# One plan and one pool layout for three phases that had one each, on one core

## The chip, the cores and the metric

The kernel runs on one core of a Trainium2 chip. The metric is device microseconds of one execution, from launch to end. The kernel before took 1201.57 us (median of 3 runs, 1199.39 to 1202.25). The engines are called TensorE (PE in the profile), VectorE (DVE), ScalarE (ACT), GpSimd (POOL) and SyncE (SP, which issues nearly all DMAs). Each engine takes its instructions strictly in the order in which the program lists them.

## The reference, cut to what matters

Linear attention with random features feeds a gated feed-forward layer. All is float32.

```
q, k, v: (8 batches, 8 heads, 576, 64);  omega: (128, 64);  q is scaled by 3.371
phi(x) = exp(h - max(h)) / sqrt(128),  h = (x/64**.25) @ omega.T - |x/64**.25|**2 / 2
kv  = phi(k).T @ v;   z = sum over positions of phi(k)
att = (phi(q) @ kv) / (phi(q) @ z + 1e-6)
x   = att as 4608 tokens x 512                       # 8 heads x 64
xn  = x / sqrt(mean(x*x) + 1e-6) * rms_g
g   = xn @ w_gate (512 x 1536);  val = xn @ w_val (512 x 1536)
out = (g * sigmoid(g) * val) @ w_out (1536 x 512)
```

## The kernel before, in words

**Number format.** The large products are made in three passes: each operand is split into a high part (a cast on ScalarE) and a low part (the difference, on VectorE or GpSimd), and TensorE adds high by high, high by low and low by high (`three_pass`, lines 147 to 154; `split`, `halve`). The weights come as 64-bit floats and are first put together from their two words (`weights` in phase A: one ScalarE and four VectorE steps for each of 36 pieces).

**Tiling.** The 4608 tokens are 36 chunks (`c`) of 128 and 12 blocks (`blk`) of 384. The 1536 hidden columns are 12 tiles (`f`) of 128.

**Phase A** (`phase_a`, lines 183 to 738) does the attention, and the first six `f` of gate and value. For each chunk `features` makes phi(k) and phi(q): load `ink` or `inq`, square and sum, project (`pjk`, `pjq`), maximum, exponentials into `kp` or `qp`. `kv_mid` and `kv_half` sum `kv`; `attend` transposes `qp` (`qt`), multiplies by `kv` (`nu`), divides, normalises, transposes (`xt`), stores the chunk in DRAM (`xn_d`, shown as `xn_scratch`) and splits it into `xT`. `gated(blk, f)` makes two products `ff` of 12 matmuls with 384 columns, gate and value, and three silu steps: `t` (tanh, ScalarE), `u` and `h` (VectorE). `u` frees the gate's PSUM bank and `h` the value's; there are two banks, so the next `ff` waits for them. `h` is stored in DRAM (`h_d`, shown as `h_scratch`). The weights of the other six `f` are combined and stored in DRAM (`lw_d`), those of `w_out` too (`wo_d`).

**Phase B** (`phase_b`, lines 741 to 970) does gate and value for the other six `f`, by a scheme with seven products in place of eight for each 2 by 2 group of blocks. `weights(un)` loads and splits seven left operands for each of six units `un` (`wr`, then `lw_un`); `tokens(bp)` loads four pieces of `xn_d` for a pair of blocks (`Xb`), takes four differences (`Xt`) and splits seven right operands (`R`); `unit` has seven products `p` of six matmuls and combines them (`c`, `u`).

**Phase C** (`phase_c`, lines 973 to 1017) multiplies all of `h_d` by `w_out`: per block and `f` a tile `hC` is loaded and split (`hh`, `hl`), and nine matmuls of 512 columns add to three banks `po`. In the first block each `w_out` tile is loaded (`oraw`, 4 buffers) and split (`ohi`, `olo`). 8 buffers for `hC`, 4 pairs for its split.

**What sets the order.** Phases A and B have a `Plan` each (lines 65 to 144): entries with an engine, an estimated duration, what they come after, a key, and the buffers that they take and give back. `order()` walks through time; a free engine takes the ready entry with the lowest key. An entry is ready 0.12 us after the last one that it needs (a DMA 2.2 us later still). `KEYS` holds the keys of the first nine chunks and the first weights. The silu steps of `gated` have the key `-1000 + 1000 + 6*blk + f`, so 0 to 71; a chunk's other steps have about its number `c`. Until the plan begins the first `ff`, a free TensorE gets `spin` matmuls. Phase C has no plan; its loop's order stands.

Each phase opens its buffers in pools of its own and closes them at its end; the next phase's pools lie in the same memory from the same end. The three lists are given to the framework under `manual_schedule` one after another (C's without it), and the framework itself places instructions of a later phase between those of an earlier one where memory and data allow.

Of the kernel before, what the change touches and what calls it, by code (L numbers as in the profile page):

```python
# [64 lines left out]
class Plan:  # L65
# [15 lines left out]
    def order(self):  # L81
# [25 lines left out]
        while len(out) < n + extra:  # L107
# [50 lines left out]
def performer_glu_kernel(  # L158
# [16 lines left out]
    with ExitStack() as ph:  # L175
        phase_a(ph, tc, qx, kx, va, vmid, omT, rmsg, wgv, wout, xn_d, h_d, lw_d, wo_d)
    with ExitStack() as ph:
        phase_b(ph, tc, lw_d, xn_d, h_d)
    with ExitStack() as ph:
        phase_c(ph, tc, wo_d, h_d, out)  # L180


def phase_a(ctx, tc, qx, kx, va, vmid, omT, rmsg, wgv, wout, xn_d, h_d, lw_d, wo_d):
    nc = tc.nc
    cpool = ctx.enter_context(tc.tile_pool(name="const", bufs=1))
# [11 lines left out]
    ve = nc.vector  # L197
    pools = {}
    slots = {}

    def pool(name, bufs, space=None, per=1):
        kw = {"space": space} if space else {}
        pools[name] = ctx.enter_context(tc.tile_pool(name=name, bufs=bufs * per, **kw))
        slots[name] = bufs

    psum = bass.MemoryType.PSUM
    wpool = ctx.enter_context(tc.tile_pool(name="wA", bufs=1))
    pool("xT", 2, per=2)
    for name, bufs in (
        ("t", 2), ("u", 2), ("h", 4), ("xr", 2), ("xn", 1), ("x", 1), ("qpT", 1), ("qp", 2),  # L210
        ("kv", 4), ("inq", 2), ("mag", 2), ("w", 4), ("sr", 1), ("f64", 2), ("ink", 3), ("v", 6),
        ("vm", 1), ("kp", 6),
    ):
        pool(name, bufs)
    pool("small", 16)
    pool("psJ", 4, psum)
    pool("psM", 2, psum)
    pool("psF", 2, psum)
    plan = Plan(slots)
    add = plan.add  # L220
    st = {}
# [10 lines left out]
    def weights(n, key):  # L232
# [65 lines left out]
        if n >= 2 * FA:  # L298

            st["wt", n] = t  # L300
            if n >= 2 * NF:
# [4 lines left out]
                i = add("SP", 0.26 / RATE, store, [i], key, land=LAND)  # L306
# [23 lines left out]
    def sums(n, key):  # L330
# [36 lines left out]
        ends.append(add("SP", 0.52 / RATE, store(2), after, key, land=LAND))  # L367
        add("NONE", 0, lambda: None, ends, give=[("w", n - 2), ("w", n), ("sr", un)])
# [163 lines left out]
    def attend(c, key):  # L532
# [126 lines left out]
        s = add("SP", 0.26 / RATE, xstore, [i], key - 0.3, land=LAND)  # L659
# [4 lines left out]
    def gated(blk, f, key):  # L664
# [34 lines left out]
        top = -1000 + key  # L699
# [9 lines left out]
        add("SP", 0.2 / RATE, store, [i], top, give=[("h", at)], land=LAND)  # L709
# [26 lines left out]
    with tc.manual_schedule():  # L736
        for begin in plan.order():
            begin()


def phase_b(ctx, tc, lw_d, xn_d, h_d):

    nc = tc.nc
    ve = nc.vector
    pools = {}
    slots = {}

    def pool(name, bufs, space=None, per=1):  # L750
        kw = {"space": space} if space else {}
        pools[name] = ctx.enter_context(tc.tile_pool(name=name + "B", bufs=bufs * per, **kw))
        slots[name] = bufs

    psum = bass.MemoryType.PSUM
    for name, bufs in (("s0", 2), ("s4", 2), ("u2", 2), ("u4", 2), ("u3", 2), ("g", 8), ("h", 6)):
        pool(name, bufs)
    lpool = ctx.enter_context(tc.tile_pool(name="lB", bufs=1))
    lw = {}
    for un in reversed(range(NU)):  # L760
        for i in range(7):
            for part in "hl":
                lw[un, i, part] = lpool.tile([P, 2, P], F32R, name=f"lw{un}_{i}{part}")
    names = ("b11", "b21", "b22", "t1", "t2", "t3", "t4")
    for nm in names:
        pool("R" + nm, 1, per=2)
    for nm in ("b11", "b21", "b22", "b12", "t1", "t2", "t4"):
        pool("X" + nm, 1)
    pool("wr", 2)
    pool("ps", 8, psum)  # L770
    plan = Plan(slots)
    add = plan.add
    st = {}

    def tile_(pool, shape, name, dtype=F32):
        return pools[pool].tile(shape, dtype, tag=pool, name=name)
# [12 lines left out]
    def weights(un, key):  # L789

        t = {}

# [10 lines left out]
        ld = add("SP", 0.39 / RATE, load(0, 3), key=key, take=[("wr", un)], land=LAND)  # L803
        ld = [ld, add("SP", 0.52 / RATE, load(3, 7), [ld], key, land=LAND - LAT)]
        ends = []
        for i, _ in ORDER:
# [6 lines left out]
                [ld[i > 2]],  # L813
# [6 lines left out]
    def tokens(bp, key):  # L820
# [3 lines left out]
        for nm, half, blk in (("b11", 0, 0), ("b12", 0, 1), ("b22", 1, 1), ("b21", 1, 0)):  # L824
# [5 lines left out]
            ld[nm] = add("SP", 0.39 / RATE, load, key=key, take=[("X" + nm, bp)], land=LAND)  # L830
# [41 lines left out]
    def unit(bp, fp, j, key):  # L872
# [31 lines left out]
        def plus(name, pool, x, y, eng=ve):  # L904
# [3 lines left out]

            return go

        out = "h" if j else "g"
        top = -1000 + key
        p = {}
        last = []
# [46 lines left out]
    for un in range(NU):  # L961
        weights(un, un)
# [120 lines left out]
```

## Time and profile before

| | |
|---|---|
| median of 3 runs | 1201.57 us |
| profiled execution, its own time | 1199.83 us |
| its span, first to last instruction | 1198.0 us |
| mean granted TensorE clock | 0.989 of full |
| TensorE busy | 1169.3 us, 98%, 7471 matmuls |
| VectorE busy | 731.4 us, 61% |
| ScalarE busy | 561.4 us, 47% |
| GpSimd busy | 193.8 us, 16% |
| DMA | 171.17 MB, 143 GB/s on average |
| first `ff` / last `ff` of phase A | 88.1 / 620.8 us |
| first `p` / last `p` of phase B | 624.3 / 890.1 us |
| first `po` / last `po` of phase C | 897.5 / 1193.4 us |

The slices of the profile (40 of 30 us) show TensorE busy 9 tenths or more nearly everywhere. The slices in which its granted clock is not full are those at 390, 540, 600, 870, 900 and 1170 us (0.89, 0.89, 0.94, 0.92, 0.96, 0.93). In the lists of groups, a line shows source line, engine, operation, output and inputs, count, busy time and mean ns, then idle time of the engine just before and who ended it. A matmul's duration is longer than its step to the next one, as matmuls are pipelined. SP is shown by the issue of its DMAs (SPq).

### The profile page before, as it was taken

The page shows a single profiled execution, that of the slowest core. Times are in us where ns is not written, and L with a number is a line of the kernel's source. Part 1 is how long each engine was busy: PE and PEld are TensorE (multiplying, and loading weights), DVE is VectorE, ACT ScalarE, POOL GpSimd, SP SyncE. Part 2 cuts the span into 40 slices and gives each one's busy share as a digit, 9 for nine tenths or more (in the row PEclk, how much of TensorE's full clock was granted, in tenths as well). Part 3 has the DMA queues.
Part 4 walks back from the last instruction along what each step waited for, and adds up shares of the span by engine and source line. Part 5 has one row for each costly group of instructions (what it writes and reads, how often), then busy time and mean ns, then how long its engine had stood idle before and what let it go on. Part 6 is the DMA issues. An engine that isn't in the chain of part 4 may idle for free.

```text
span 1198.0 us, 20303 instructions
## 1 busy us (share of the span) xinstructions
PE 1169.3 (98%) x7471; PEld 1079.6 (90%) x7471; DVE 731.4 (61%) x1483; ACT 561.4 (47%) x1382; POOL 193.8 (16%) x221
## 2 busy tenths in 40 slices
PE   9999999999999899998989999999979999999998
PEld 6889999999999899998989999999978888888886
DVE  5877898898888355456325878877755333333332
ACT  5778677766766345454226442442424222222221
POOL 0232121120101012110119422331310000000000
PEclk9999999999999899998999999999999999999999
DMA  8755487586664423223214322322137444444441
GB/s 296 227 169 174 151 266 256 196 260 210 228 206 163 138 80 111 80 85 117 74 40 156 100 86 93 104 83 85 54 104 238 126 125 121 133 143 121 124 125 67
DMA packets 98035, 171.17 MB, mean 143 GB/s; under 512 B 9360, under 2 KB 65552, under 8 KB 97936
## 3 DMA queue, kind: packets, MB, share of 16 engines
q1 hardware_dynamic: 97712, 169.58, 43.9%
q8 instruction: 59, 0.97, 0.3%
q10 hardware_dynamic: 224, 0.30, 0.1%
q14 instruction: 40, 0.33, 0.1%
HBM read 114.00 MB, written 55.84 MB: 142 GB/s over the span
## 4 chain that ended last, share of the span: by engine, by line
PE 48%; issue 3%; POOL 1%; DMA 0%; DVE 0%; ACT 0%; POOLq 0%; SPq 0%; ACTq 0%; DVEq 0%
PE po L152 8%; PE po L153 8%; PE po L154 8%; PE p L154 6%; PE p L153 6%; PE p L152 6%; PE ff L152 2%; PE ff L154 2%; PE ff L153 2%; POOL c L907 0%; DMA oraw<-wo_scratch 0%; PE nu L558 0%; POOL Rt2l L785 0%; DMA h_scratch<-h 0%; POOL Rt4l L785 0%
## 5 line engine op out<-in xcount | busy, mean ns | idle before, releaser
L152 PE MATMUL ff<-xhi,whi 128*128 128x384 f32 x576 | 204.1, 354 | 9.4 <-DVE u L685 9.4
L154 PE MATMUL ff<-xhi,wlo 128*128 128x384 f32 x576 | 194.7, 338 | 0.0
L153 PE MATMUL ff<-xlo,whi 128*128 128x384 f32 x576 | 194.6, 338 | 0.0
L57 DVE TENSOR_TENSOR hl<-hC,hh 128x384 fp32r<-128x384 f32 x144 | 80.2, 557 | 184.4 <-ACT hh L54 183.9
L152 PE MATMUL po<-ohi,hh 128*128 128x512 f32 x432 | 168.2, 392 | 7.0 <-ACT ohi L54 7.0
L153 PE MATMUL po<-olo,hh 128*128 128x512 f32 x432 | 168.1, 391 | 0.0
L154 PE MATMUL po<-ohi,hl 128*128 128x512 f32 x432 | 168.1, 391 | 0.0
L54 ACT CAST hh<-hC 128x384 fp32r<-128x384 f32 x144 | 74.3, 516 | 195.8 <-PE po L153 179.4
L152 PEld LDWEIGHTS ff<-xhi,whi 128*128 128x128 f32 x576 | 109.8, 191 | 11.7 <-DVE u L685 10.2
L153 PEld LDWEIGHTS ff<-xlo,whi 128*128 128x128 f32 x576 | 110.1, 191 | 0.0
L154 PEld LDWEIGHTS ff<-xhi,wlo 128*128 128x128 f32 x576 | 109.6, 190 | 0.0
L152 PEld LDWEIGHTS po<-ohi,hh 128*128 128x128 f32 x432 | 81.8, 190 | 24.5 <-ACT ohi L54 7.3
L153 PEld LDWEIGHTS po<-olo,hh 128*128 128x128 f32 x432 | 81.5, 189 | 17.0
L154 PEld LDWEIGHTS po<-ohi,hl 128*128 128x128 f32 x432 | 81.5, 189 | 16.9
L428 ACT ACTIVATE qp<-pjq,biq 128x128 f32<-128x128 f32 x288 | 88.2, 377 | 17.7 <-DVE biq L419 15.1
L428 ACT ACTIVATE kp<-pjk,bik 128x128 f32<-128x128 f32 x288 | 89.1, 378 | 15.4 <-DVE bik L419 14.9
L938 ACT ACTIVATE c<-c 128x384 f32<-128x384 f32 x72 | 37.6, 526 | 112.9 <-DVE c L907 95.7
L691 DVE SCALAR_TENSOR_TENSOR h<-u,ff 128x384 f32<-128x384 f32 x72 | 39.8, 552 | 56.1 <-PE ff L154 55.0
L681 ACT ACTIVATE t<-ff 128x384 f32<-128x384 f32 x72 | 35.6, 495 | 79.9 <-PE ff L154 79.7
L558 PE MATMUL nu<-kv,qpT 128*128 128x65 f32 (+1 forms) x640 | 71.6, 264 | 0.0
L558 PEld LDWEIGHTS nu<-kv,qpT 128*128 128x128 f32 (+1 forms) x640 | 69.0, 182 | 2.9 <-issue 0.9
L907 DVE TENSOR_TENSOR c<-p,u 128x384 f32<-128x384 f32 x108 | 58.9, 551 | 19.5 <-PE p L154 19.4
(145 smaller groups left out, 2364.2 us busy)
## 6 DMA issues: line engine op xcount, KB each, us to landing
hC<-h_scratch SPq DMA_DIRECT2D x144, 192.0 KB, 2.4
ink<-in_kx_dram SPq DMA_DIRECT2D x36, 512.0 KB, 4.5
inq<-in_qx_dram SPq DMA_DIRECT2D x36, 512.0 KB, 4.1
h_scratch<-h SPq DMA_DIRECT2D x72, 192.0 KB, 1.9
h_scratch<-c SPq DMA_DIRECT2D x72, 192.0 KB, 1.8
f<-in_wgv_dram SPq DMA_DIRECT2D x24, 512.0 KB, 4.6
xn_scratch<-xr SPq DMA_DIRECT2D x36, 256.0 KB, 2.7
Xb<-xn_scratch SPq DMA_DIRECT2D x24, 384.0 KB, 3.2
```

The lines of the kernel that those rows point to most:

```text
L54: nc.scalar.copy(hi, raw)
L57: lo_eng.tensor_tensor(out=lo, in0=raw, in1=hi.bitcast(F32), op=ALU.subtract)
L152: nc.tensor.matmul(out, lhsT=ah, rhs=bh, start=first, stop=False)
L153: nc.tensor.matmul(out, lhsT=ah, rhs=bl, start=False, stop=False)
L154: nc.tensor.matmul(out, lhsT=al, rhs=bh, start=False, stop=last)
L428: nc.scalar.activation(st[tag + "p", c][:, h, :], t["pts"][h % 2][:, h // 2, :], AF.Exp, bias=t["bi"][:, h : h + 1], scale=SCALE,)
L558: nc.tensor.matmul(pt[lo:hi, i, :], lhsT=t["qpT"][:, h, lo:hi], rhs=st["kv", b][:, h, :], start=True, stop=True,)
L681: nc.scalar.activation(t["t"], t[0], AF.Tanh, scale=0.5)
L691: ve.scalar_tensor_tensor(out=t["h"], in0=t["u"], scalar=0.5, in1=t[1], op0=ALU.mult, op1=ALU.mult)
L907: eng.tensor_tensor(out=t[name], in0=t[x], in1=t[y], op=ALU.add)
L938: nc.scalar.activation(t[nm], t[nm], AF.Silu)
```

## The change

One function with one plan holds all three phases. The pools are in groups (`GROUPS`); a group opens and closes by an entry of the plan on an engine of its own, `POOLS`, that takes no time. Groups named in `RIGHT` lie at the other end of SBUF.

- At the start `late`, `psA` (PSUM) and, on the other side, `early` are open. `early` has what the attention and the weights need (`f64`, `w`, `ink`, `inq`, `kp`, `qp`, `v`, ...), `late` what the silu steps and `xT` need.
- `to_b`, after the last user of `early`: `early` closes; `operands` (the seven `R`, and the left operands of unit 0, `lw0`) and `sources` (`X`, `wr`) open on the same side. B's loads and the splits of `R` and of unit 0 come after `to_b`.
- `in_b`, after all entries of A: `psA` and `late` close; `products` and `psB` open. The left operands of units 1 to 5 lie there.
- `to_c`, after the last user of `sources`: `first` opens (6 `hC` buffers, 3 pairs for its split, 2 for raw `w_out`, the split tile of `f` = 0). C's loads and these splits come after `to_c`.
- `in_c`, after all entries of A and B: `products` and `psB` close; the other split `w_out` tiles, the output buffers and `psC` open.

In phase C `wst` has 2 buffers (4 before), `hin` 6 (8), the split pairs 3 (4). C is planned too; its keys are `12000 + 12*blk + f`. B's keys begin at 6000. The silu steps get keys near -2000, below all others. The plan makes an entry ready at once when all that it needs ran on its own engine (and for `POOLS`). `KEYS` are new. The arithmetic and the shapes of all instructions stay.

```diff
-    "k": [-24.0, -20.7, -17.6, -7.8, -8.5, -5.1, 2.5, -6.7, 2.6],
-    "q": [-11.3, -7.1, 2.6, 2.9, 3.8, 3.9, 4.1, 4.6, 6.3],
-    "w": [
-        -1.5, -1.6, -2.7, 3.0, 6.2, 6.0, 6.5, 5.7,
-        11.7, 11.0, 13.1, 11.0, 34.5, 20.9, 13.7, 38.5,
-    ],
-    "lead": 6.14,
-    "v": 1.16,
-    "kv": 0.77,
-    "attend": -8.69,
+    "k": [-23.5, -21.2, -13.7, -12.7, -11.4, -10.9, -7.9, -5.4, -2.9],
+    "q": [-19.0, -9.9, -1.7, -1.2, 1.9, 4.5, 4.6, 5.1, 5.8],
+    "w": [-6.9, 1.8, -0.5, 3.1, 4.2, 4.5, 4.5, 4.7, 5.0, 5.2, 6.1, 9.3, 10.1, 6.5, 19.1, 35.5],
+    "lead": 4.94,
+    "v": 2.67,
+    "kv": -9.77,
+    "attend": -12.63,
 }
+GROUPS = {
...
+    "first": {"hin": (6, 1), "hs": (3, 2), "wst": (2, 1), "wo0": (1, 1)},
...
+RIGHT = ("early", "operands", "sources", "first")
...
-                if done < 0:
-                    continue
-                given.update(self.items[i][6])
-                for u in users[i]:
+                if done >= 0:
+                    given.update(self.items[i][6])
+                for u in users[i] if i >= 0 else ():
+                    at_once = self.items[u][0] in ("POOLS", self.items[i][0])
+                    if (at_once and (not self.items[i][7] or self.items[u][0] == "POOLS")) != (done < 0):
+                        continue
...
+    def change(after, old, new, then=lambda: None):
+        def go():
+            for group in old:
+                leave(group)
+            for group in new:
+                enter(group)
+            then()
+        return add("POOLS", 0, go, after)
...
-        top = -1000 + key
+        top = -3000 + key
...
+    to_b = change(users("early"), ["early"], ["operands", "sources"], lambda: left_tiles(0))
+    in_b = change(
+        list(range(to_b)),
+        ["psA", "late"],
+        ["products", "psB"],
+        lambda: [left_tiles(n) for n in range(1, NU)],
+    )
...
+        ready = to_b if un == 0 else in_b
...
-                [ld[i > 2]],
+                [ld[i > 2], ready],
...
+            after = [st["xs", NC * (2 * bp + blk) + i] for i in range(NC)] + [to_b]
+            ld[nm] = add("SP", 0.39 / RATE, load, after, key, [("X" + nm, bp)], land=LAND)
...
+    to_c = change(users("sources"), ["sources"], ["first"])
+    in_c = change(list(range(to_c)), ["psB", "products"], ["last", "psC"])
+    def out_weights(f, key):
...
+        ready = [in_c if f else to_c]
+        i = add("SP", 0.26 / RATE, load, [st["wo", f], to_c], key, [("wst", f)], land=LAND)
+        raw = lambda: t["raw"]
+        st["o", f] = halve("DVE", hi, lambda: hi("l"), raw, key, [i] + ready, DM, give=[("wst", f)])
...
+        i = add("SP", 0.2 / RATE, load, [st["hs", at], to_c], key, [("hin", at)], land=LAND)
+        i = halve("DVE", hi, lambda: t["l"], lambda: t["raw"], key, [i], TB, [("hs", at)], [("hin", at)])
+        take = [("psO", blk, c) for c in range(NC)] if f == 0 else []
+        before = [st["made"]] if "made" in st else []
+        i = add("PE", 2.06, product, before + [i, st["o", f], in_c], key, take, [("hs", at)])
```

## Rows read from the trace of the kernel before

**Rows 1.** Waits of TensorE: total us, times, longest us.
```profile
PE ff L152 <- DVE u L685: 9.4, 2, 5.4
```
**Rows 2.** Windows: length, busy us of PE, PEld, DVE, ACT, POOL; PEclk, DMA, GB/s.
```profile
405.00:410.00 5.00, 4.87 (x15) 4.87 (x16) 1.10 (x3) 0.01 (x1) 0.00 (x0) 0.50 0.11 39
```
**Rows 3.** Timeline of TensorE at 400: start, us, instruction [idle before <-releaser].
```profile
400.86 0.34 PE L154 MATMUL ff<-xhi,wlo 128*128 128x384 f32 x1
405.13 0.69 PE L152 MATMUL ff<-xhi,whi 128*128 128x384 f32 x1 [3.94 <-DVE u L685]
...
410.74 0.34 PE L154 MATMUL ff<-xhi,wlo 128*128 128x384 f32 x1
```
**Rows 4.** Timeline of TensorE at 550.
```profile
548.42 1.00 PE L558 MATMUL nu<-kv,qpT 128*128 128x65 f32 x8
554.84 0.69 PE L152 MATMUL ff<-xhi,whi 128*128 128x384 f32 x1 [5.42 <-DVE u L685]
...
560.88 0.36 PE L153 MATMUL ff<-xlo,whi 128*128 128x384 f32 x1
```
**Rows 5.** Timeline of TensorE from A to B.
```profile
620.84 0.34 PE L154 MATMUL ff<-xhi,wlo 128*128 128x384 f32 x1
624.33 0.45 PE L152 MATMUL p<-Rb11h,lw_0h 128*128 128x384 f32 x1 [3.15 <-ACT lw_0h L780]
...
631.34 0.33 PE L152 MATMUL p<-Rt2h,lw_4h 128*128 128x384 f32 x1
```
**Rows 6.** Timeline of TensorE from B to C.
```profile
890.13 0.34 PE L154 MATMUL p<-Rt4h,lw_2l 128*128 128x384 f32 x1
897.48 1.65 PE L152 MATMUL po<-ohi,hh 128*128 128x512 f32 x3 [7.02 <-ACT ohi L54]
...
905.97 0.39 PE L152 MATMUL po<-ohi,hh 128*128 128x512 f32 x1
...
908.01 0.39 PE L152 MATMUL po<-ohi,hh 128*128 128x512 f32 x1
```
**Rows 7.** Timeline of SP (issues) and of ScalarE, 390 to 404.
```profile
391.15 1.74 SPq L828 DMA_DIRECT2D Xb<-xn_scratch  x4
...
394.85 0.34 SPq L378 DMA_DIRECT2D inq<-in_qx_dram  x1
...
402.97 0.63 ACT L382 ACTIVATE inq<-inq 128x512 f32<-128x512 f32 x1 [4.38 <-DMA inq<-in_qx_dram]
```
**Rows 8.** Timeline of ScalarE, 543 to 551.
```profile
543.83 0.82 ACT L780 CAST Rb11h<-Xb 128x768 fp32r<-128x768 f32 x1
...
550.39 0.49 ACT L681 ACTIVATE t<-ff 128x384 f32<-128x384 f32 x1
```
**Rows 9.** Timeline of TensorE at 88, and the group of `spin` in the list by line.
```profile
88.16 0.42 PE L152 MATMUL ff<-xhi,whi 128*128 128x384 f32 x1
...
L713 PE MATMUL spin<-ones 128*128 128x512 f32 x135 | 42.8, 456 | 1.5 <-POOL ones L193 1.5
```
**Rows 10.** Tiles `u`, `Xb`, `lw_0l`: ns min/median/max, first and last start.
```profile
L685 DVE SCALAR_TENSOR_TENSOR u<-t,ff x72: 541/553/556, 92.1 to 617.6; 128x384 f32<-128x384 f32 x72
...
L785 DVE TENSOR_TENSOR Rb22l<-Xb,Rb22h x6: 948/2326/2331, 553.4 to 851.1; 128x768 fp32r<-128x768 f32 x6
...
L785 POOL TENSOR_TENSOR lw_0l<-wr,lw_0h x6: 732/738/741, 624.4 to 654.6; 128x256 fp32r<-128x256 f32 x6
```
**Rows 11.** Windows: the tail of A.
```profile
570.00:600.00 30.00, 30.00 (x184) 29.76 (x183) 10.72 (x21) 8.29 (x17) 5.33 (x7) 1.00 0.21 67
```
**Rows 12.** Tile `oraw`: its splits, and the landing of its loads.
```profile
L54 ACT CAST ohi<-oraw x12: 613/620/623, 896.8 to 912.5; 128x512 fp32r<-128x512 f32 x12
L57 DVE TENSOR_TENSOR olo<-oraw,ohi x12: 684/692/695, 897.5 to 913.1; 128x512 fp32r<-128x512 f32 x12
...
DMA to landing us min/median/max: 2.8/4.5/5.1
```
**Rows 13.** A weight's longest step in the list by line.
```profile
L272 DVE SCALAR_TENSOR_TENSOR w<-f,mag 128x512 int32<-128x512 int32 x36 | 27.5, 767 | 0.1
```

More of the change, by code (lines that the diff above doesn't have):

```diff
@@ L174, in performer_glu_kernel, with enter, leave, users @@
 ):
[L175 to L183, printed above, removed]
-    nc = tc.nc
-    cpool = ctx.enter_context(tc.tile_pool(name="const", bufs=1))
+    nc = tc.nc
+    ve = nc.vector
+    pools = {}
+    stacks = {}
+    plan = Plan({name: bufs for group in GROUPS.values() for name, (bufs, _) in group.items()})
+    add = plan.add
+    st = {}
+    def enter(group):
+        stack = stacks[group] = ExitStack()
+        side = "right" if group in RIGHT else "left"
+        space = {"space": bass.MemoryType.PSUM} if group.startswith("ps") else {}
+        for name, (bufs, per) in GROUPS[group].items():
+            pools[name] = stack.enter_context(
+                tc.tile_pool(name=name, bufs=bufs * per, side=side, **space)
+            )
+    def leave(group):
+        stacks.pop(group).close()
+    def change(after, old, new, then=lambda: None):
[6 more added lines that the diff above has]
+        return add("POOLS", 0, go, after)
+    def users(*groups):
+        names = {name for group in groups for name in GROUPS[group]}
+        return [
+            n for n, it in enumerate(plan.items) if any(t[0] in names for t in it[5] + it[6])
+        ]
+    for group in ("late", "early", "psA"):
+        enter(group)
+    cpool = wpool = pools["keep"]
     ident = cpool.tile([P, P], F32, name="ident")
@@ L196, in phase_a @@
     nc.scalar.dma_start(om[D:P, :], omT)
[L197 to L221, printed above, removed]
     def tile_(pool, shape, name, dtype=F32, tag=None):
@@ L735, in phase_a, with left_tiles @@
             gated(blk, f, 1000 + blk * FA + f)
[L736 to L758, printed above, removed]
     lw = {}
-    for un in reversed(range(NU)):
+    def left_tiles(un):
+        pool = pools["lw0" if un == 0 else "lw"]
         for i in range(7):
             for part in "hl":
[L763 to L776, printed above, removed]
+                lw[un, i, part] = pool.tile([P, 2, P], F32R, name=f"lw{un}_{i}{part}")
+    to_b = change(users("early"), ["early"], ["operands", "sources"], lambda: left_tiles(0))
[4 more added lines that the diff above has]
+        lambda: [left_tiles(n) for n in range(1, NU)],
+    )
     def halve(eng, hi, lo, raw, key, after, size, take=(), give=(), name=None):
@@ L787, in halve, with left @@
         return add(eng, dur, low, [h], key, give=give)
-    def weights(un, key):
+    def left(un, key):
         t = {}
+        ready = to_b if un == 0 else in_b
         def load(a, b):
@@ L869, in tokens @@
             st["R", bp, nm] = e
-            add("NONE", 0, lambda: None, [e] + [d[x] for x in users.get(nm, [])], give=[("X" + src, bp)])
+            add("NONE", 0, lambda: None, [e] + [d[x] for x in readers.get(nm, [])], give=[("X" + src, bp)])
     def unit(bp, fp, j, key):
@@ L892, in mm @@
         def mm(n, i, nm, after):
-            deps = after + ([st["l", un, i]] if bp == 0 else []) + [st["R", bp, nm]]
+            deps = after + ([st["l", un, i], in_b] if bp == 0 else []) + [st["R", bp, nm]]
             give = [("R" + nm, bp)] if un == NU - 1 else []
-            return add("PE", 1.045, product(n, i, nm), deps, key + 0.01 * n, [("ps", at, n)], give)
+            if not after and st.get("last"):
+                deps = deps + [st["last"]]
+            st["last"] = len(plan.items)
+            return add("PE", 1.045, product(n, i, nm), deps, key + 0.01 * n, [("psB", at, n)], give)
         def copy(n):
@@ L958, in unit @@
                 )
-                add("SP", 0.2 / RATE, store, [i], top, give=[("h", at, nm)], land=LAND)
+                at_d = 2 * bp + (nm[2] == "2"), FA + 2 * fp + (nm[1] == "2")
+                st["hs", at_d] = add(
+                    "SP", 0.2 / RATE, store, [i], top, give=[("hB", at, nm)], land=LAND
+                )
+    base = 6000
+    for bp in range(NBLK // 2):
+        right(bp, base + NU * bp - 0.5)
     for un in range(NU):
-        weights(un, un)
-    for bp in range(NBLK // 2):
-        tokens(bp, 0.5 + NU * bp - (bp > 0) - (bp == 0))
+        left(un, base + un)
@@ new lines, in out_tile, with load, hi, product @@
+    def out_tile(blk, f, key):
+        t = {}
+        at = (blk, f)
+        def load():
+            t["raw"] = tile_("hin", [P, TB], f"hC{blk}_{f}")
+            nc.sync.dma_start(t["raw"], h_d[blk, :, f])
+        def hi():
+            if "h" not in t:
+                t["h"] = tile_("hs", [P, TB], f"hh{blk}_{f}", F32R)
+                t["l"] = tile_("hs", [P, TB], f"hl{blk}_{f}", F32R)
+            return t["h"]
+        def product():
+            if f == 0:
+                st["po"] = [tile_("psO", [P, DM], f"po{blk}_{c}") for c in range(NC)]
```

137 lines of the change are left out of this document (82 added, 55 removed).

## The prediction

> **What bounds the kernel now.** I read four views, in this order. The page's busy line and its slices (table above) say that TensorE is the bound: busy 98% of the span, at full clock in most slices. So the time is TensorE's own work, plus the places where it has none. Second, the waits of TensorE: of the few long ones, two lie inside phase A, both behind the silu step `u` [rows 1], and one stands at the start of each later phase. Third, the timeline around each. I price a hole as the time from the moment at which the next matmul was due to the first one back at full rate, less what the matmuls between would have taken at full rate, 0.173 us each (0.227 in C). That counts the slow restart too: after the first hole the granted clock is 0.50 of full, the lower level of 1.2 GHz, and the matmuls take 0.52 us instead of 0.33 [rows 2, 3].
>
> The four:
> - Hole 1 [rows 3]: due at 401.03, back at 410.74, 17 matmuls (2.95 us) between: 9.71 - 2.95 = 6.8 us.
> - Hole 2 [rows 4]: the eight `nu` matmuls end at about 549.3; back at 560.88 with 13 matmuls and eight small ones (3.15 us) between: 8.4 us.
> - A to B [rows 5]: due at 621.02, back at 631.34, 18 matmuls (3.12 us) between: 7.2 us.
> - B to C [rows 6]: due at 890.30, back at 905.97, 27 matmuls (6.12 us) between: 9.5 us.
>
> The full-rate step is 0.1733 us for a matmul of 384 columns (B's last 1493 steps, from 631.34 to 890.13) and 0.227 for one of 512 (9 in 2.04 us, the last two of [rows 6]). Together 31.9 us. As a check, B has 1512 matmuls, 262.1 us at 0.1733, and lasts from 621.0 to 890.3, which is 269.3: 7.2 more, all of it at its start. C has 1296, 293.8 us, and lasts 303.3: 9.5 more, at its start too.
>
> Fourth, what lies before the holes on the other queues. Hole 1: SP issued four loads of `Xb` and two of `wr`, which belong to phase B, at 391 to 394, and only then the `inq` load that phase A needed. It landed at 402.97; ScalarE stood in its queue at the square of `inq`, with the `t` step of the waiting `ff` behind it [rows 7]. Hole 2: six casts of phase B's right operands stand before the `t` step on ScalarE (run at 550.39), and subtractions of phase B before `u` on VectorE, so that the `ff` starts at 554.84 [rows 4, 8]. Both holes are phase B's preparation, put into A's queues where A didn't allow for it.
>
> **The head.** TensorE reaches its first `ff` at 88.16; until then it fills gaps with 135 `spin` matmuls, 42.8 us of busy time without work [rows 9].
>
> **The change part by part.**
> *One plan for all three phases.* B's loads and splits are now entries of A's plan, with keys above 6000 and only after all users of the `early` pools (the last `inq`, `qp`, weights). By then no `inq` load is left to be pushed back, so hole 1 goes: -6.8. Hole 2 goes in its present form, as the `t`, `u`, `h` steps are taken first whenever they are ready (keys near -2000). What stays is an entry begun just before: one cast of 0.82 us on ScalarE and one subtraction of 0.95 (the shortest of its group) on VectorE [rows 8, 10]. A silu step has about 0.8 us to spare: 12 matmuls at 0.173 are 2.08, and the chain to the release of PSUM is `t` 0.49, `u` 0.55 [rows 8, 10] and what is estimated at 0.25 between them. So a double collision costs up to 0.95 us, a single one 0.15. The preparation is 7 casts, 4 differences and 7 subtractions; I take 1.5 us in all. Bounds: 0, if none collide, and 8.4, if hole 2 comes back. Room is there: at 570 to 600 VectorE was busy 10.7 of 30 us and ScalarE 8.3 [rows 11], and the 11 entries of about 0.95 (10.5 us) fit between. If that cover is gone, they stand before B's first products (rival 4). -8.4 + 1.5.
>
> One rule bears on this. [Rows 10] show that a subtraction of B's stretches to 2.33 us where GpSimd works beside it, while a silu step (`u`) never took more than 0.556 us. The Trainium skill, "SBUF — State Buffer", section "Who interferes with whom", says that a VectorE instruction with two SBUF inputs blocks against a GpSimd instruction that reads SBUF, and one with at most one SBUF input does not. By that rule `left(0)`'s seven GpSimd subtractions, now in A's tail, could stretch seven entries by up to the GpSimd instruction's 0.74 us each, and with a silu step behind each the sum would lose up to 5 us more; by the rows of `u` alone, nothing. I keep 1.5, and the loss within the bound of 8.4.
>
> *A to B.* `lw0` and the right operands lie on the other side, over the `early` pools, so the cast `lw_0h` for which the first product waited [rows 5] no longer stands behind the last `h` store. B's first product is next on TensorE behind the last `ff`; its PSUM bank has been free since the last projections. Unit 1's left operand must lie over A's left side and so starts after A: seven GpSimd subtractions at 0.74 us [rows 10] are 5.2 us, against the 42 matmuls of unit 0, 7.28. That fits, with one `c` of GpSimd's between. 7.2 becomes 0.3 (bounds 0 and 7.2): -6.9.
>
> *B to C.* `first` opens when B's sources are done (their last reader on VectorE begins at 851.1, [rows 10]), so three `h` tiles and `wo0` are split before B ends. The first `f` starts at once; its 2.04 us cover the last VectorE steps of B, and then `wo1`'s pair is due, which can only be written after B's pools close: about 0.6 us late. After that a new wait appears: raw weights have 2 buffers instead of 4. One buffer's round is issue 0.34 [rows 7], landing 2.8 to 4.5, cast 0.62, subtraction 0.69 [rows 12] plus an estimated 0.2: 4.7 to 6.3 us, for two `f` of TensorE, 4.08. Over five rounds that is 3 to 11 us, less the two tiles that lie ready. Loads are then hardly crowded (six `h` tiles are in), so I take the row of the shortest landing, and 3 us in all; bounds 0.6 and 11. 9.5 becomes 3.0: -6.5. Four pairs of `hs` becoming three costs nothing while TensorE is the bound: cast and subtraction of a tile are about as long as those of `wo` [rows 12], 1.3 us, and have the 4.08 of two `f`.
>
> *New keys in the head.* `q2` moves from 2.6 to -1.7, ahead of two raw weights (`w1`, `w2`); a weight has four VectorE steps, the longest 0.77 us [rows 13], so up to 3.1 us each, and I take 2.4; kv and attend steps jump further ahead. That can bring the first `ff` some 5 us sooner; but block 0 then wants its weights at the same rate. The trace doesn't show the new order. Bounds: 15 us gained (about a third of the spins) and 8 lost (three weights); I take 4 gained, nearest to the two weights moved. *Same-engine successors without the 0.12 us delay* in the plan change only the order: 0, within these bounds.
>
> **Sum.** -6.8 - 6.9 - 6.9 - 6.5 - 4.0 = -31.1 us on the profiled execution's 1199.83 (span 1198.0, 1.83 around it): 1168.7. The median of the three runs is 1.74 above that execution: 1170.5.
>
> **Rivals.**
> 1. *The collision stays*: preparation still sits before a silu step in strictly ordered queues, because the plan's landing times are too early. For: hole 1 was one landing of 8.1 us; against: the loads come when A's are over. One hole of 8.4 in place of 1.5: 1177.
> 2. *C's first block is starved by two raw buffers*: 10 us instead of 3: 1177.5. For: the landing of 4.5 [rows 12]; against: that was under a burst.
> 3. *Slower: the head's new order starves A.* Once the first `ff` has begun there are no spins, so each missing weight or `x` makes a hole with a slow restart: (6.8 + 8.4) / 2 = 7.6 us. Without the head's gain 27.1 us are won; from four holes (30.4) on the kernel isn't faster, and five give 1201.6 - 27.1 + 38 = 1212. For: an earlier start with weights at 4.9 us of VectorE per 4.2 us of `ff`; against: TensorE had no hole from 88 to 400 in the old order.
> 4. *The early opening doesn't come early* (the change doesn't do what it says): the `early` pools end only with A. Then a landing of about 3 us and 18 entries of 0.8 to 0.95, 11 of them on VectorE (10.5 us), stand before and within the first unit, with a slow restart: about 16 us in place of 0.3: 1186. Against: in the old kernel B's first cast ran 77 us before A's last `ff` [rows 5, 8], so the memory under it was free.
> 5. *The head gains 15*: 1159.5.
>
> **Chances.** Forecast 0.47 (its own range 1164 to 1177), rivals 1 and 2 0.12 each, 3 0.12, 4 0.06, 5 0.11. Range: 1157 to 1191, which leaves out rival 3 and the ends. About 0.3% can be told from no change. Faster by more: 0.88; rival 3 split by its number of holes gives 0.05 within and 0.07 slower.
>
> **What would show it.** Right: no wait of `ff` for `u` over 2 us; no B load on SP before the last `inq`; first `p` within 0.5 us of the last `ff`; first `po` within 0.5 us of the last `p`, at full clock; small repeated waits of `po` for `ohi` in block 0. First `ff` at about 84. Wrong: several holes of `ff` before 400, with half clock after each; a first `ff` beyond 96; `lw_0h` still behind an `h` store.

## The result, and the profile after

The kernel after takes 1207.42 us (median of 17 runs, 1198.06 to 1209.82); the kernel before, run beside it, takes 1200.80 (17 runs, 1199.2 to 1202.25). The ratio is 1.0042, 95% interval 1.0026 to 1.0059: slower by 0.4%, where 1170.5 and a gain of 2.6% were forecast. The profiled execution of after takes 1208.84 us, its span 1206.9. Medians and ratios leave out executions in a slower state, such as one of e3's six (1658.8 us, at a granted clock of 0.645).

What the prediction looked at came out nearly as it said: 34.4 us gained where 31.1 were forecast. The first fence of after answers to [rows 1]: the list of TensorE's waits (total us, times, longest us).

```profile
PE p L180 <- DVE Rt3l L793: 16.6, 5, 4.7
PE p L179 <- DVE c L920: 3.3, 1, 3.3
PE ff L179 <- DVE u L719: 1.9, 2, 1.1
...
PE po L179 <- ACT oh L788: 1.5, 1, 1.5
```

The 9.4 us for `u` are 1.9, in two waits of 0.8 and 1.1; so holes 1 and 2 [rows 3, 4] are gone. The wait of 1.1 is a collision of the kind that the prediction priced: a subtraction of B's is stretched while GpSimd works, another stands behind it, and `u` comes after both (the timelines of VectorE and TensorE in after):

```profile
546.38 2.05 DVE L793 TENSOR_TENSOR Rt2l<-Xt,Rt2h 128x768 fp32r<-128x768 f32 x1
548.36 0.94 DVE L793 TENSOR_TENSOR Rt1l<-Xt,Rt1h 128x768 fp32r<-128x768 f32 x1
549.23 0.54 DVE L719 SCALAR_TENSOR_TENSOR u<-t,ff 128x384 f32<-128x384 f32 x1
549.82 0.44 PE L179 MATMUL ff<-xhi,whi 128*128 128x384 f32 x1 [1.08 <-DVE u L719]
```

But the two longest waits are new, and both lie inside phase B. The places of [rows 5, 6, 9] in after, on the timeline of TensorE:

```profile
77.05 0.42 PE L179 MATMUL ff<-xhi,whi 128*128 128x384 f32 x1
...
598.76 0.34 PE L181 MATMUL ff<-xhi,wlo 128*128 128x384 f32 x1
599.79 0.41 PE L179 MATMUL p<-Rb11h,lw_0h 128*128 128x384 f32 x1 [0.70 <-issue]
...
895.94 0.34 PE L181 MATMUL p<-Rt4h,lw_2l 128*128 128x384 f32 x1
896.98 0.47 PE L179 MATMUL po<-oh,hh 128*128 128x512 f32 x1 [0.70 <-issue]
```

The group of `spin` in the list by line:

```profile
L747 PE MATMUL spin<-ones 128*128 128x512 f32 x97 | 32.0, 472 | 1.5 <-POOL ones L251 1.5
```

Phase A ends at 598.76 instead of 620.84; the changes of phase take 1.0 us from matmul to matmul instead of 3.5 and 7.4. Phase B, which took 273.2 us from its first product to phase C's, takes 297.2, and phase C 305.2 instead of 295.9 (last `po` at 1202.21 and 1193.38). Windows over the phases (length; busy us of PE, PEld, DVE, ACT, POOL; granted clock, DMA share, GB/s), the kernel before:

```profile
621.00:897.50 276.50, 264.46 (x1515) 263.13 (x1513) 199.82 (x328) 111.46 (x225) 100.42 (x93) 0.99 0.29 93
897.50:1194.00 296.50, 296.27 (x1296) 244.77 (x1296) 101.50 (x179) 85.66 (x166) 0.00 (x0) 0.99 0.43 132
```

and after:

```profile
600.00:898.00 298.00, 277.40 (x1517) 274.75 (x1517) 204.44 (x328) 108.48 (x219) 97.64 (x86) 0.97 0.26 87
898.00:1203.00 305.00, 302.93 (x1293) 242.71 (x1291) 100.09 (x176) 84.46 (x164) 0.00 (x0) 1.00 0.42 125
```

In phase B the granted clock is lower and TensorE stands idle for 20 us; in phase C the clock is full and TensorE nearly always busy, and yet 9 us more pass. So there are two losses of different kinds.

**Loss 1, at the boundaries of the block pairs.** TensorE at the second boundary of after:

```profile
704.02 0.33 PE L181 MATMUL p<-Rt1h,lw_3l 128*128 128x384 f32 x1
704.20 0.34 PE L179 MATMUL p<-Rt3h,lw_5h 128*128 128x384 f32 x1
707.53 0.69 PE L180 MATMUL p<-Rt3l,lw_5h 128*128 128x384 f32 x1 [3.00 <-DVE Rt3l L793]
708.01 0.52 PE L181 MATMUL p<-Rt3h,lw_5l 128*128 128x384 f32 x1
```

and VectorE there:

```profile
701.75 4.39 DVE L958 TENSOR_TENSOR c<-c,c 128x384 f32<-128x384 f32 x3
706.07 0.54 DVE L920 TENSOR_TENSOR u<-p,s 128x384 f32<-128x384 f32 x1
706.53 0.94 DVE L793 TENSOR_TENSOR Rt3l<-Xb,Rt3h 128x768 fp32r<-128x768 f32 x1
```

The low part `Rt3l` is made 3 us late, behind three products of gate and value. Then comes a slow restart like that of [rows 2], as a window of TensorE shows (length, busy us, granted clock, DMA); behind the wait of 3.0 us at 804 the clock stays full:

```profile
707.60:709.60 2.00, 2.00 (x6) 0.50 0.94 269
807.20:810.60 3.40, 3.37 (x19) 1.00 0.98 275
```

In the kernel before, at its first boundary, VectorE had `Rt3l` done at 671.6,

```profile
670.68 0.95 DVE L785 TENSOR_TENSOR Rt3l<-Xb,Rt3h 128x768 fp32r<-128x768 f32 x1
```

and TensorE wanted it at 675.2; the new pair's first products with `Rt2`, `Rt1` and `Rt3` stand 2.08 us apart there, with others between:

```profile
670.86 0.33 PE L152 MATMUL p<-Rt2h,lw_4h 128*128 128x384 f32 x1
...
672.94 0.33 PE L152 MATMUL p<-Rt1h,lw_3h 128*128 128x384 f32 x1
...
675.02 0.33 PE L152 MATMUL p<-Rt3h,lw_5h 128*128 128x384 f32 x1
675.20 0.33 PE L153 MATMUL p<-Rt3l,lw_5h 128*128 128x384 f32 x1
```

In after they stand 1.04 apart (702.12, 703.16, 704.20). One wait more, 3.3 us at 621, has the same neighbour: one such product on VectorE

```profile
615.17 8.68 DVE L958 TENSOR_TENSOR c<-c,c 128x384 f32<-128x384 f32 x1
```

lasts 8.68 us beside a row of GpSimd's subtractions for the left operands (and one sum `c`), which stand 0.70 apart and end here:

```profile
615.49 0.74 POOL L793 TENSOR_TENSOR lw_0l<-wr,lw_0h 128x256 fp32r<-128x256 f32 x1
616.18 0.75 POOL L793 TENSOR_TENSOR lw_1l<-wr,lw_1h 128x256 fp32r<-128x256 f32 x1
...
622.69 0.74 POOL L793 TENSOR_TENSOR lw_2l<-wr,lw_2h 128x256 fp32r<-128x256 f32 x1
```

**Loss 2, the step.** Matmuls start further apart where nothing waits. In windows of equal length at full clock, the columns being PE busy (x matmuls), granted clock, DMA: the kernel before, phase B,

```profile
725.00:750.00 25.00, 25.00 (x146) 1.00 0.18 64
```

and after:

```profile
725.00:750.00 25.00, 25.00 (x144) 1.00 0.15 50
```

For 80 us of phase C (with PEld, DVE, ACT too), before,

```profile
920.00:1000.00 80.00, 80.00 (x354) 66.25 (x353) 5.50 (x8) 2.35 (x4) 1.00 0.44 132
```

and after:

```profile
930.00:1010.00 80.00, 80.00 (x343) 64.41 (x343) 4.12 (x6) 1.76 (x3) 1.00 0.42 124
```

From start to start (mean of the steps without a wait or a slow clock) that is 0.1763 us instead of 0.1733 for `p`, 0.2338 instead of 0.2267 for `po`. Unit 0 and `f` = 0, for which both operands lie on the right side, keep the old steps (medians 0.173 and 0.227). On the left side (`lw`, `wo`) tiles start at 128 modulo 512 bytes, as everything did in the kernel before; on the right side (`R`, `hs`, `lw0`, `wo0`) at 480. No trace shows addresses; these places are reckoned from the layout of the pools.

Where the time went, on the profiled executions:

| | forecast | measured |
|---|---|---|
| holes 1 and 2 and the head, until the last `ff` | -17.7 | -22.1 |
| A to B | -6.9 | -6.2 (7.2 to 1.0) |
| B to C | -6.5 | -6.1 (9.5 to 3.4) |
| inside B | 0 | +34.2 |
| inside C | 0 | +9.1 |
| sum | -31.1 | +8.9 |

Inside B: 297.18 - 1512 x 0.1733 = 35.15, less 0.86 in the change to C and 0.1 at the start. Of it 20.9 are in six steps of over 0.5 us (the waits), 9.0 in steps of 0.2 to 0.5 us, nearly all of them slow restarts behind the first four of the six waits, and 4.3 in longer steps. Inside C all 9.1 are longer steps. The restarts differ from run to run: the 17 runs have mean granted clocks from 0.997 (the fastest, 1198.06 us) to 0.989, and the longer runs are those with the lower clock. The profiled run, at 0.991, is one of the longer ones.

### The profile page after: what moved, and what is told of

Read it like the earlier page. It is cut to its first block, busy times and chain, and to the rows that moved or that the text cites. A ratio compares the mean times of both kernels' runs of the same rounds, so it can differ in the third digit from the quotient of the medians.

```text
span 1206.9 us, 20240 instructions
## 1 busy us (share of the span) xinstructions
PE 1174.7 (97%) x7433; PEld 1078.6 (89%) x7433; DVE 736.8 (61%) x1483; ACT 561.5 (47%) x1382; POOL 202.5 (17%) x221
## 4 chain that ended last, share of the span: by engine, by line
PE 48%; DVE 4%; ACT 1%; POOL 1%; issue 1%; DMA 1%; ACTq 0%; DVEq 0%
PE po L180 8%; PE po L181 8%; PE po L179 8%; PE p L180 7%; PE p L181 7%; PE p L179 6%; DVE c L958 2%; PE ff L179 1%; PE ff L181 1%; PE ff L180 1%; DVE u L920 0%; DVE Rt3l L793 0%; DMA h_scratch<-h 0%; DVE c L920 0%; DMA h_scratch<-c 0%
## 5 line engine op out<-in xcount | busy, mean ns | idle before, releaser
L179 PE MATMUL po<-oh,hh 128*128 128x512 f32 x432 | 171.2, 396 | 2.1 <-ACT oh L788 1.5
L180 PE MATMUL po<-ol,hh 128*128 128x512 f32 x432 | 171.3, 396 | 0.2 <-DVE ol L793 0.2
L181 PE MATMUL po<-oh,hl 128*128 128x512 f32 x432 | 171.1, 396 | 0.0
L661 POOL TENSOR_TENSOR xlo<-xr,xhi 128x512 fp32r<-128x512 f32 x36 | 47.4, 1317 | 323.1 <-ACT xhi L658 323.1
L179 PEld LDWEIGHTS po<-oh,hh 128*128 128x128 f32 x432 | 81.3, 188 | 22.4 <-ACT oh L788 1.9
L180 PEld LDWEIGHTS po<-ol,hh 128*128 128x128 f32 x432 | 81.3, 188 | 20.7 <-DVE ol L793 1.2
L181 PEld LDWEIGHTS po<-oh,hl 128*128 128x128 f32 x432 | 81.3, 188 | 19.5
L462 ACT ACTIVATE kp<-pjk,bik 128x128 f32<-128x128 f32 x288 | 79.8, 388 | 18.9 <-DVE bik L453 14.2
L920 POOL TENSOR_TENSOR c<-s,s 128x384 f32<-128x384 f32 x36 | 41.3, 1148 | 174.1 <-ACT s L913 160.7
L719 DVE SCALAR_TENSOR_TENSOR u<-t,ff 128x384 f32<-128x384 f32 x72 | 39.6, 551 | 49.0 <-ACT t L715 48.6
```

What stands on the lines that cost most here:

```text
L179: nc.tensor.matmul(out, lhsT=ah, rhs=bh, start=first, stop=False)
L180: nc.tensor.matmul(out, lhsT=ah, rhs=bl, start=False, stop=False)
L181: nc.tensor.matmul(out, lhsT=al, rhs=bh, start=False, stop=last)
L462: nc.scalar.activation(st[tag + "p", c][:, h, :], t["pts"][h % 2][:, h // 2, :], AF.Exp, bias=t["bi"][:, h : h + 1], scale=SCALE,)
L661: nc.gpsimd.tensor_tensor(out=st["xT", blk][1][:, :, cs], in0=t["xr"], in1=st["xT", blk][0][:, :, cs].bitcast(F32), op=ALU.subtract,)
L719: ve.scalar_tensor_tensor(out=t["u"], in0=t["t"], scalar=1.0, in1=t[0], op0=ALU.add, op1=ALU.mult)
```

## The experiments

"Excess of B" below is the time from the first `p` to the first `po`, less 1512 x 0.1733 us. Steps are means from start to start, of steps under 0.2 us (`p`) and 0.26 us (`po`).

| run | median us | ratio to before | excess of B | `p`, `po` step |
|---|---|---|---|---|
| before | 1200.80 | | 11.1 | 173.3, 226.7 ns |
| after | 1207.42 | 1.0042 [1.0026, 1.0059] | 35.2 | 176.3, 233.8 |
| e1: 32 bytes on the right | 1208.05 | 1.0063 [1.0048, 1.0078] | 34.5 | 173.5, 233.0 |
| e2: delay back | 1203.64 | 1.0019 [1.0006, 1.0032] | 31.2 | 176.3, 233.7 |
| e3: low parts off GpSimd | 1196.12 | 0.9967 [0.9955, 0.9980] | 22.2 | 176.3, 233.8 |
| e4: before, 32 bytes in C | 1208.43 | 1.0070 [1.0053, 1.0087] | 12.8 | 173.3, 233.3 |
| e5: chain out | 1202.77 | 1.0020 [1.0008, 1.0032] | 29.5 | 176.3, 233.8 |
| e6: chain out, delay back | 1181.49 | 0.9846 [0.9830, 0.9861] | 8.3 | 176.3, 233.8 |
| e7: order written out | 1182.05 | 0.9839 [0.9818, 0.9860] | 9.6 | 176.3, 233.8 |
| e8: 352 bytes on the right | 1194.44 | 0.9960 [0.9940, 0.9979] | 33.8 | 173.4, 226.7 |
| e9: e6 and 352 bytes | 1168.16 | 0.9734 [0.9718, 0.9751] | 2.0 | 173.4, 226.8 |
| e10: e6 and 96 bytes | 1167.64 | 0.9729 [0.9715, 0.9744] | 2.0 | 173.3, 226.8 |
| e11: e6 and 224 bytes | 1180.64 | 0.9830 [0.9814, 0.9846] | 9.7 | 176.1, 232.9 |
| e12: e9 and e3 | 1168.68 | 0.9740 [0.9722, 0.9757] | 6.3 | 173.3, 226.8 |

**e1, the offset of the right side.** A filler moves the right side's tiles down by 32 bytes; every engine's order stays.

```diff
+    side = ctx.enter_context(tc.tile_pool(name="side", bufs=1, side="right"))
+    filler = side.tile([P, 8], F32, name="filler")
+    nc.gpsimd.memset(filler, 0.0)
```

> The changed kernel with 32 bytes of filler at the outer end of the second side, so that every tile on that side starts at a multiple of 64 bytes, as those on the first side do in phases B and C; the order on every engine stays, but for the one instruction that clears the filler. Theory offset (a matmul's step is longer where its two operands start at different offsets modulo 64 bytes): the step of po falls from 0.234 to 0.227 us for f 1 to 11, that of p from 0.176 to 0.173; 1188 x 7.4 ns in C and some 4 us in B: 12 to 13 us less, about 1195. Rival side (the step is longer because the operands lie at opposite ends of the memory): steps and time stay, 0.234 and about 1207.

Half right. B's step is back at 0.173 (0.3 us in long steps instead of 4.3), C's is not: 0.233. The waits cost 1.2 us more and the restarts in B 2.2 more: here the granted clock falls behind all six waits, and once more at the start of C. So the time stays. The offset decides in B; for C this left it open.

**e2, the planner's delay for same-engine successors** comes back behind phase A.

```diff
-                    at_once = self.items[u][0] in ("POOLS", self.items[i][0])
+                    at_once = self.items[u][0] == "POOLS" or (
+                        self.items[u][0] == self.items[i][0] and u < self.edge
+                    )
...
+    plan.edge = to_b
```

> The changed kernel, with the old 0.12 us delay back in the plan between entries of one engine from phase B on. Theory order (in B the same-engine followers, the gate times value products, now go ahead of the subtraction Rt3l): the five waits of p for Rt3l go, 16.6 us, and with the slow matmuls after them 20 to 25: about 1184. Rival port (what makes Rt3l late is that those products take 2 us in place of 0.55 beside GpSimd's subtractions): they stay long, p still waits for Rt3l, over 1200.

The wait for `Rt3l` goes, and another late low part takes its place. TensorE's waits:

```profile
PE p L183 <- DVE Rb22l L797: 12.9, 5, 4.3
PE p L182 <- DVE c L924: 3.1, 1, 3.1
```

The time, 1203.6, is the one forecast by "port", but the wait is another than it said; "order" had 1184. The order on VectorE chooses which operand is late, not whether one is.

**e3, GpSimd's subtractions.** The low parts of `lw1` to `lw5` and of `Rt2`, `Rb21`, `Rt4` are made on VectorE.

```diff
-                "POOL",
+                "DVE" if un else "POOL",
...
-                "POOL" if bp and nm in ("t2", "b21", "t4") else "DVE",
+                "DVE",
```

> The changed kernel, with the low parts of units 1 to 5's left operands and of the right operands t2, b21, t4 made on VectorE in place of GpSimd. Theory port: no gate times value product is over 0.6 us (longest now 8.68), the wait of p at 621 (3.3 us) goes, and the waits for Rt3l shrink by the 3 to 4 us that the products were stretched, so nearly to nothing: about 1180 to 1185. Rival order: VectorE has 0.95 us more before Rt3l at each pair of blocks, the five waits stay at 3 us or more: 1203 to 1212.

The group of the products of gate and value in the list by line, 600 to 900 (busy us, mean ns), in after:

```profile
L958 DVE TENSOR_TENSOR c<-c,c 128x384 f32<-128x384 f32 x72 | 60.8, 875 | 1.4 <-POOL c L920 1.1
```

and in this run:

```profile
L958 DVE TENSOR_TENSOR c<-c,c 128x384 f32<-128x384 f32 x72 | 37.4, 552 | 0.3
```

Its waits of TensorE in B:

```profile
PE p L180 <- DVE Rt1l L793: 7.0, 5, 1.4
PE p L180 <- DVE Rb22l L793: 4.0, 5, 0.8
PE p L180 <- DVE Rt4l L793: 1.7, 5, 0.4
```

The longest now takes 0.667 us (8.68 in after) and the wait at 621 is gone, so in this order that one is GpSimd's doing. The boundaries still wait, 2.5 us each, in pieces of at most 1.4 us, and the granted clock stays at 1.00. The time lies between the two forecasts: GpSimd is part of the loss, not its root.

**e4, the offset alone, in the kernel before.** Its phase C gets a filler of 32 bytes ahead of `hs`; all orders stay.

```diff
+    off = pool("offC", 1).tile([P, 8], F32, name="off")
+    nc.gpsimd.memset(off, 0.0)
```

> The kernel before, with 32 bytes of filler ahead of the split h tiles of phase C, so that they start 32 bytes off a multiple of 64 and the w_out tiles on one; both stay on the one side, and the order on every engine stays but for the clearing of the filler. Theory offset: the step of po rises from 0.227 to 0.234 for all f: 1296 x 7.4 ns, 9.6 us more, about 1210. Rival side: 0.227, about 1201.

```profile
920.00:1000.00 80.00, 80.00 (x345) 64.40 (x344) 4.61 (x7) 1.76 (x3) 1.00 0.41 124
```

The 354 matmuls of 80 us become 345, with both operands' tiles opened from one side. So moving one operand's tiles by 32 bytes is enough to make the step longer, without the sides, the orders or anything else of the change.

**e5, e6, e7: TensorE's order.** The diff of the change also holds an edit that the prediction passed over: in `mm`, a unit's first product comes after the previous unit's last one (`st["last"]`). In the kernel before, TensorE went p3 of unit u, p0 of u+1, p4 of u, p1 of u+1, p5 of u, p2 of u+1, p6 of u; in after it goes unit by unit. Either way an operand's first use in a pair of blocks comes seven products after its last use in the pair before. But unit by unit, the seven operands come free and are wanted one product (1.04 us) apart; interleaved, two. e5 takes the chain out; e6 also brings the delay back as in e2; e7 keeps all of after's planner, but writes TensorE's old order out. e6's order is not quite the old one, as its expectation has it: two units run side by side, operands again two products apart, but the first use comes eleven products after the last, not seven. Only e7 changes the pace alone.

```diff
-            if not after and st.get("last"):
-                deps = deps + [st["last"]]
-            st["last"] = len(plan.items)
```

> The kernel after without the dependency that lets a unit's first product start only behind the previous unit's last one; the planner's other new rule (an instruction's successor on the same engine is ready at its end) stays. On TensorE only the boundaries of the block pairs come out otherwise: three products of the next pair's unit 1 go in ahead of p3 of unit 0; inside a pair the units still stand one after the other. Theory 'rate': at a boundary seven right operands have to be rewritten within one unit (7.3 us) because the old pair's last unit gives them free, and the new pair's first unit wants them, at one product's distance; this kernel hardly changes that, except that each late operand is waited for with three products of other work in hand: the five waits for Rt3l move to another operand or shrink by at most half, 1198 to 1208. Rival 'chain': any permission to run past a late operand suffices: the five waits (16.7 us in all) vanish, 1188 to 1193. Rival 'GpSimd' (VectorE is held by GpSimd's subtractions): nothing changes, 1205 to 1209.

> The kernel after without that dependency and with the planner's delay behind an instruction back for same-engine successors in the second and third phase. TensorE's units then interleave two by two (p2 of unit 4, p1 of unit 5, p3 of unit 4, p2 of unit 5, ...), as in the kernel before. Theory 'rate': operands come free, and are wanted, at two products' distance over 14.6 us, so VectorE keeps up: waits of TensorE for R operands under 4 us in five boundaries together (now 16.6 and 12.9 with the delay alone), their slow restarts (9 us) gone too, the second phase's excess over 1512 x 0.1733 us from 35 to 12 to 16 (the long steps of 4.3 us and the wait at 621 of 3.3 stay), 1184 to 1190. Rival 'GpSimd': VectorE is late because GpSimd's subtractions hold it, whatever TensorE's order: waits stay over 10 us, 1200 to 1206.

e7 in place of the chain:

```diff
+            st["p", bp, un, n] = len(plan.items)
...
+            turn += [(x, 3), (y, 0), (x, 4), (y, 1), (x, 5), (y, 2), (x, 6)]
...
+    for a, b in zip(ids, ids[1:]):
+        it = list(plan.items[b])
+        it[3] = it[3] + (a,)
+        plan.items[b] = tuple(it)
```

> The kernel after with TensorE's order of products written out as in the kernel before (p3 of unit u, p0 of u+1, p4 of u, p1 of u+1, p5 of u, p2 of u+1, p6 of u), and everything else of after's planner kept, the same-engine successors without delay too. Theory 'rate': as the run with the old rules, waits for R operands under 4 us together, 1184 to 1190. Rival 'at once': VectorE's chain of additions goes ahead of the operands' low parts because its successors are ready at once, so waits stay at 8 to 17 us, 1198 to 1208. Rival 'GpSimd': the same 1200 to 1206, with VectorE instructions stretched over 2 us at the moment of each wait.

TensorE's waits in B, e5:

```profile
PE p L180 <- DVE Rt3l L793: 11.4, 5, 3.6
PE p L179 <- DVE c L917: 3.1, 1, 3.1
```

e6:

```profile
PE p L182 <- ACT lw_0h L792: 2.0, 1, 2.0
```

e7:

```profile
PE p L179 <- DVE u L918: 1.3, 1, 1.3
PE p L180 <- DVE Rb22l L793: 0.9, 1, 0.9
```

"Rate" holds, and "chain" and "at once" fall: in e5 the planner still sets the units one after the other, with three products exchanged at each boundary, and five waits stay; in e7 the units interleave, successors have no delay, and the five waits are gone as in e6. "GpSimd" falls as a sufficient cause: in e7 `Rb22l` still takes 2.07 us in the mean (0.95 undisturbed), and TensorE waits for it 0.9 us in all; one product of gate and value is held for 8.90 us there, and the wait behind it is 1.3 us (3.3 in after). Both runs are 2 to 3 us better than the lower end expected.

**e8, the distance 0.** As e1 with 352 bytes (`[P, 88]`): both sides at 128 modulo 512.

> The kernel after with a filler of 352 bytes at the right side's outer end, so that tiles of the right side and of the left side start at the same place modulo 512 bytes (128); every engine's order is unchanged. Theory 'offset beyond 64': the third phase's step depends on the distance of the two operands' starts modulo more than 64 bytes (with a filler of 32 bytes, distance 320 modulo 512, it was still 0.2333 while the second phase's was back at 0.173): steps of po at 0.227 for all f, excess of the third phase over 1296 x 0.227 under 2 us (now 9), of the second phase's long steps under 1 us (now 4.3), 1193 to 1197. Rival 'something else of the third phase' (the sides, the DMAs that write hs, the stores): po stays at 0.233, 1203 to 1208 as with the 32 bytes.

```profile
930.00:1010.00 80.00, 80.00 (x355) 66.28 (x354) 4.13 (x6) 1.76 (x3) 1.00 0.43 127
```

Both steps are back at their old values, and 13.0 us with them; long steps are 4.1 us less in B and 9.1 in C, as the table of losses has it. Only the right side's tiles moved, and the two operands still lie on two sides, so the rival falls. The waits of B stay (17.0 us for `Rt3l`).

**e9 to e12, both causes together.** e9 is e6 with e8's filler; e10 and e11 have 96 and 224 bytes, distances 256 and 128; e12 is e9 with e3's edit. All four have e6's order, with its eleven products, and not the old one.

> The kernel after with the planner's old rules in the second and third phase (TensorE's units interleave) and the filler of 352 bytes (both sides' tiles start alike modulo 512 bytes). If the two causes are apart from each other, their gains add: 1181.5 for the old rules, less the long steps that are still in it, 4.5 us in the second phase and 9.1 in the third: 1168 (1165 to 1171); steps 0.173 and 0.227. If the faster steps only uncover another engine (VectorE in the second phase), waits of TensorE for operands come back and the time is 1172 to 1180.

> As the run with old rules and 352 bytes, but with a filler of 96 bytes: right-side tiles start at 384 modulo 512, left-side ones at 128, distance 256. If the steps want the operands alike only modulo 256 or 128: 0.173 and 0.227, 1168, as with 352. If they want them alike modulo 512: 0.227 to 0.235 in the third phase for all f but the first, 1177 or more. Seen so far in the third phase: distance 0 0.227, 32 0.2333, 320 0.2333, 352 0.234; in the second: 0 and 320 0.173, 352 0.176.

> As the same with a filler of 224 bytes: right-side tiles at 256 modulo 512, left-side ones at 128, distance 128. If the steps want the operands alike only modulo 128: 0.173 and 0.227, 1168. If modulo 256 or 512: 0.233 in the third phase, 1177 or more; the second phase at 0.173, as at distance 320, which is no multiple of 128.

> As the run with old rules and 352 bytes, and with the low parts of the left operands 1 to 5 and of the right operands t2, b21, t4 on VectorE, not on GpSimd. Theory: with the units interleaved VectorE has time to spare, and what GpSimd's subtractions hold up no longer reaches TensorE: within 2 us of the run with GpSimd, 1166 to 1170. Rival 'GpSimd still costs': the product of two SBUF tiles, which beside GpSimd's subtractions takes up to 8.7 us, still delays something, 1160 to 1165. Rival 'VectorE is now full': it takes over 50 subtractions and TensorE waits for it, 1171 to 1185.

The gains add: 1207.42 - 25.93 (e6) - 12.98 (e8) = 1168.5, measured 1168.16. e9's phases, as windows:

```profile
600.00:864.00 264.00, 262.87 (x1513) 261.94 (x1513) 200.46 (x327) 111.21 (x219) 92.32 (x86) 1.00 0.30 98
864.00:1161.00 297.00, 294.89 (x1296) 242.83 (x1296) 100.67 (x178) 84.96 (x164) 0.00 (x0) 1.00 0.43 129
```

At distance 256 the steps are as at 0; at 128 they are not. Here are e10's phase C, at 256, and e11's, at 128:

```profile
930.00:1010.00 80.00, 80.00 (x354) 66.26 (x354) 4.12 (x6) 1.76 (x3) 1.00 0.43 126
930.00:1010.00 80.00, 80.00 (x345) 64.45 (x344) 4.12 (x6) 1.76 (x3) 1.00 0.42 124
```

e11's expectation of 0.173 for `p` was a miss: 0.176. In e12 the products of gate and value take 0.551 us in the mean (0.718 in e9), and TensorE gains nothing: with the units interleaved GpSimd's hold costs nothing any more, and e3's 11.3 us were a part of the same loss. e12's larger excess of B is one wait of 3.6 us for `lw_0h`, which e9 doesn't have.

e9 and e10 beat both kernels: 2.7% faster than before.

## Why the prediction was wrong

- **Holes 1 and 2**: right. Of the 1.5 us taken for collisions one wait of 1.1 shows, and of the kind named: `u` stands behind a subtraction of B's that GpSimd stretches to 2.05 us, and behind one more. `u` itself took 0.556 us at most, as [rows 10] had it. Rivals 1 and 4 did not come.
- **The head**: right in sign, too small. The first `ff` comes 11.1 us earlier, at 77 instead of the 84 named, with 97 `spin` for 135. 4.2 of that are given back: 22.1 - 15.2 (the two holes) leaves 6.9, where 4.0 were taken. Of the 4.2, 1.9 are the two waits for `u`; the rest is not traced one by one, but 16 `pjk` matmuls more than before now stand behind the first `ff`. Rival 3, the only one on the slower side, did not come either: no hole of `ff` exceeds 1.1 us.
- **A to B, B to C**: right within 0.7 and 0.4 us. What is left is 0.86 us at each change, most of it "issue" (0.70), and the wait of 1.5 for `oh` at the third phase's start. The 3.4 us of B to C are near the 3.0 taken partly by luck: the pair for `f` = 1 came later than the 0.6 named, and the small repeated waits for raw weights, most of the 3.0, did not come; the two buffers (rival 2) starve nothing.
- **The step that failed** is "*Same-engine successors without the 0.12 us delay* in the plan change only the order: 0, within these bounds", and beside it the silence on `st["last"]`. The sum took B's inside from the kernel before, where it had no excess, though both of the edits that give B its order change it. An order is not free where it sets the pace at which buffers come free and are wanted again: the 0 measured +34.2 us inside B (4.3 of them in the longer steps, below), e7 gives back 25.4 by TensorE's order alone, and e2 and e5 show that neither edit undone alone gives more than 4.7. The 0.07 for a slower kernel stood on rival 3, starvation in the head, which did not come; that the kernel is slower has another cause.
- **The price of GpSimd's hold on VectorE** was looked up for seven subtractions in A's tail only. In B, the place to look was the first unit's products beside the left operands' subtractions: 3.3 us of wait. The Trainium skill, "SBUF — State Buffer", section "Who interferes with whom", says that a VectorE instruction with two SBUF inputs contends with a GpSimd instruction that reads SBUF, and that one with at most one, outside the modes that use two ports, doesn't. The trace agrees for both kinds: 8.68 us for `c*c`, 0.556 for `u`.
- **The unspoken assumption** that TensorE's steps stay at 0.1733 and 0.227 us, a second term put at 0. The diff moves every tile, and the moved distance between the two operands of a matmul costs 13.0 us (e8).

Without these two losses the change does what was forecast of it: e9, which keeps the holes closed, the head and the phase changes, takes 1168.2 us. That the number lies near 1170.5 does not save the prediction, which was of the change as it stands.

## What to carry to other kernels

When a phase is put under another plan, compare the bottleneck engine's order in its steady part before and after, and ask of buffers that stand single at which pace they come free and are wanted again, for that pace is what the refilling engines must keep. Here an operand's last use and its next first one stood seven products apart in both orders; the pace, one product or two, decided. When tiles move, look at the plain step of matmuls in a stretch without waits first: the changes of 2 and 3% seen there came from the addresses, not from the schedule.

## What the runs showed of the hardware that was not expected

- The step of matmuls depends on the distance between the starts of the two operands' tiles. By distance modulo 512 bytes, with 512 columns: 0.227 us at 0 and 256; 0.233 at 32, 128 and 320; 0.234 at 352. With 384 columns: 0.173 at 0, 256 and 320; 0.176 at 128 and 352. As 0 and 256 come out alike, the pattern may repeat every 256 bytes; that, the reason, and other distances were not tried.
- A VectorE product of two SBUF tiles took 8.68 us, until 623.85, beside GpSimd instructions of 0.74 to 1.01 us one behind the other, the last from 622.69 to 623.43: it did not get in between two of them. e7 has another such product, of 8.90 us; in e3, without that row, the longest takes 0.667.
- In after, of six waits of 3 to 5 us the first four are followed by slow restarts, at the lower level of the clock, that cost 1.7 to 2.9 us each; behind the last two, of 3.0 us, the granted clock stays at 1.00. In e1 it falls behind all six. So a wait of this length did not cost a restart each time. In e3, fifteen waits of up to 1.4 us leave the mean granted clock at 1.00.
